# Column sums in a Sinkhorn loop: two 256-column products of split operands in place of one fp32 product

## The chip, the core and the metric

One core of a Trainium2 chip runs the whole kernel. The metric is the device time in microseconds, the median of several runs. The core has five engines that run side by side, each its own queue in order: TensorE (PE; its weight loads are shown apart as PEld), VectorE (DVE), ScalarE (ACT), GpSimd (POOL) and SyncE (SP), which issues transfers. SBUF is the on-chip memory; TensorE writes to PSUM, which VectorE and ScalarE read.

## What is computed

A linear attention feeds a first mixture of experts (soft slots), and that a second one, whose gates a Sinkhorn loop evens out. The change touches only the loop:

```python
def _moe2_ref(x, w_gate, w1, w2):
    N, D = x.shape                      # 2304 tokens, 512 features
    E = w_gate.shape[1]                 # 8 experts
    logits = x @ w_gate
    P = np.exp(logits - logits.max())
    for _ in range(8):
        P /= P.sum(1, keepdims=True) + 1e-09     # rows
        P /= P.sum(0, keepdims=True) + 1e-09     # columns
        P *= N / E
    out = np.zeros((N, D))
    for e in range(E):
        h = np.maximum(x @ w1[e], 0.0)
        out += P[:, e:e + 1] * (h @ w2[e])
    return out
```

## The kernel before

The second mixture is TensorE's long part. It goes through 8 experts, and in each through 9 blocks of 256 tokens (the loop over `blocks`, L1247). A block of an expert is 7 products (`product`, L1170, the seven of a fast scheme for block matrices), each of 12 matmuls with a 256-column moving operand, and behind the third product the first layer of the next block: 4 matmuls into PSUM tile `z1`, then 4 into `z0` (`first_layer`, L1077). `hidden` (L1088) makes the seven operands of the next block from these two tiles in five steps, one behind each product: ScalarE and VectorE form sums and rounded parts (`s`, `hh_s`, `hh_a`, `hl_a`), and GpSimd forms the rests of four sums (`lo_s`, L1107: `hl_s`, 128x512, two pairs a block). `take` (L1189) adds the finished products into `xo`; in the first expert ScalarE copies some of them and VectorE adds the others. GpSimd also prepares the next expert's weights (`w_t`, `w_b`, `moe_w`, 128x1024, by the tables `W_SUMS` and `W_PARTS`, L1243): one such operation stands behind the sixth step of most blocks, after the second pair of `hl_s`.

The gates `P` stand in SBUF as 128 partitions x 18 token tiles x 8 experts. They are wanted only when the first expert ends, so the Sinkhorn loop (`sinkhorn`, L1021) is a generator whose steps are strewn into the first expert's blocks: `SINK_0` for block 0 and `SINK` for the others (L1245). With `SINK = {1: 3, 5: 2}` one pass of the loop spans two blocks: behind product 5 (counted from 0) of a block VectorE multiplies `P` by the reciprocal row sums and reduces it over its 18 tiles to `cs`, 128x8. Behind product 1 of the next block TensorE adds `cs` over the partitions and repeats the sum on all of them by a product with a matrix of ones (L1067, PSUM tile `pcs`); VectorE reads it, inverts, multiplies `P` and takes the next row sums. Pass 0 has its row and column sums at the end of block 0, in one stretch. The tile `pcs` is the buffer of `z0` in passes 0 to 6. In pass 7 the next expert's `make_stack` and `spread_stack` (L991, L1009) fall in the same block: TensorE makes `ps`, VectorE splits it into `st` (a copy and a subtraction), and TensorE spreads it by the products `pr` just ahead of `pcs`.

What sets the order is the program text: all engines are wrapped in `InOrder` (L43), so each queue runs its instructions as the code names them. `gst` (L1220, 128x8, rounded fp32) holds the gate's operand, which is used up when the loop begins; `pad` (L477) is an unused tile of 8 elements.

Of the kernel before, what the change touches and what calls it, by code (L numbers as in the profile page):

```python
# [7 lines left out]
F32 = mybir.dt.float32  # L8
F32R = mybir.dt.float32r
AF = mybir.ActivationFunctionType  # L10
ALU = mybir.AluOpType
# [7 lines left out]
E, SPE, FF = 8, 4, 1024  # L19
# [35 lines left out]
def tile_kernel(ctx: ExitStack, tc: tile.TileContext, a):  # L55
    nc = tc.nc
    PE, V, A, G, SP = nc.tensor, nc.vector, nc.scalar, nc.gpsimd, nc.sync

    const = ctx.enter_context(tc.tile_pool(name="const", bufs=1, side="left"))
# [8 lines left out]
    def load_const(name, shape, pool=None, q=SP):  # L68
        t = (pool or const).tile(shape, F32, name=name, bufs=1)
        q.dma_start(out=t, in_=a[name])  # L70
        return t
# [62 lines left out]
    def load_k(t):  # L134
        x = kp.tile([128, 512], F32, tag="kt", name=f"kt{t}", bufs=4)
        SP.dma_start(out=x, in_=a["kT"][t])
        kt_t[t] = x
# [336 lines left out]
    load_k(2)  # L474
    load_v(1)
    load_k(3)
    const.tile([128, 8], F32, name="pad", bufs=1)  # L477
    wg = const.tile([128, KC, E], F32, name="wg", bufs=1)
    ct4 = const.tile([128, 256], F32R, name="ct4", bufs=1)
    ident = load_const("ident", [128, 128])  # L480
    ones = load_const("ones", [128, 128])
# [16 lines left out]
    PE, V, A, SP, G = (InOrder(tc, x) for x in (PE, V, A, SP, G))  # L498
# [189 lines left out]
    def old_sums(c):  # L688
# [14 lines left out]
        out=dg, in0=ident[0:NS, 0:NS].unsqueeze(1).to_broadcast([NS, 3, NS]), scalar1=mx[0:NS], scalar2=-1.0,  # L703
# [18 lines left out]
    for h in range(2):  # L722
        ps = mm(f"psit{h}", (F0, P1)[h])
        for c in range(2):
            for n in range(2):
                for g in range(2):
                    r = slice(g * 64, (g + 1) * 64)
                    PE.matmul(
                        ps[r, c * NS:(c + 1) * NS], x_t[NT - 2 + n][:, h * 256 + c * 128:h * 256 + (c + 1) * 128][:, r], ee[:, n, :],
                        start=c + n == 0, stop=n == 1, skip_group_check=True,  # L730
# [220 lines left out]
    for g in range(4):  # L951
        r = slice(32 * g, 32 * g + 32)
# [25 lines left out]
    cp = ctx.enter_context(tc.tile_pool(name="cp", bufs=1, side="right", reuse_waits="tile"))  # L978
# [6 lines left out]
    def acc_tile(name):  # L985
        return pm.tile([128, 512], F32, tag="m", name=name)

    def z_tile(n, name):
        return pz.tile([128, 1024], F32, tag=f"z{n}", name=name)
# [31 lines left out]
    def sinkhorn():  # L1021

        pg = acc_tile("pgate")
        for c in range(KC):
            for g in range(2):
                r = slice(g * 64, (g + 1) * 64)
                PE.matmul(pg[r, 0:8 * E].rearrange("p (r e) -> p r e", r=8), sot[:, c, r], wg[:, c, :].unsqueeze(1).to_broadcast([128, 8, E]), start=c == 0, stop=c == KC - 1)
        V.tensor_copy(out=gst, in_=pg[:, 0:E])
        V.tensor_tensor(out=gst[64:128, :], in0=pg[64:128, 0:E], in1=gst[64:128, :].bitcast(F32), op=ALU.subtract)
        yield  # L1030
        pl = acc_tile("plog")
        for t in range(NT):
            PE.matmul(
                pl[:, t * E:(t + 32) * E].rearrange("p (r e) -> p r e", r=32),
                ct[t // 4][:, t % 4 * 128:(t % 4 + 1) * 128], gst.unsqueeze(1).to_broadcast([128, 32, E]),
                start=True, stop=True, skip_group_check=True,
            )
            if t in (7, 13):
                yield
        yield  # L1040
        V.tensor_copy(out=P, in_=pl[:, 0:NT * E].rearrange("p (t e) -> p t e", e=E))
        gm, gm1 = gmt[:, 0:1], gmt[0:1, 1:2]
        V.tensor_reduce(out=gm, in_=pl[:, 0:NT * E], axis=AX.X, op=ALU.max)
        G.memset(PE1[:, :, E:E + 1], 1e-9)
        yield
        pg = acc_tile("pgm")
        PE.transpose(pg[0:1, 0:128], gm, ident)
        V.tensor_reduce(out=gm1, in_=pg[0:1, 0:128], axis=AX.X, op=ALU.max)
        yield
        PE.matmul(pg[:, 128:129], ones[0:1, :], gm1, start=True, stop=True)  # L1050
        yield
        V.tensor_scalar_mul(gm, pg[:, 128:129], -1.0)
        A.activation(out=P, in_=P, func=AF.Exp, bias=gm)
        yield
        for it in range(8):
            rs = cp.tile([128, NT, 1], F32, tag="rs", name=f"rs{it}")
            V.tensor_reduce(out=rs, in_=PE1, axis=AX.X, op=ALU.add)
            V.reciprocal(out=rs, in_=rs)
            yield
            V.tensor_tensor(out=P, in0=P, in1=rs.to_broadcast([128, NT, E]), op=ALU.mult)  # L1060
            yield
            cs = cp.tile([128, 1, E], F32, tag="cs", name=f"cs{it}")
            csf = cs.rearrange("p o e -> p (o e)")
            V.tensor_reduce(out=csf, in_=P.rearrange("p t e -> p e t"), axis=AX.X, op=ALU.add)
            yield
            pg = z_tile(0, f"pcs{it}") if it < 7 else acc_tile(f"pcs{it}")
            PE.matmul(pg[:, 0:E], ones, csf, start=True, stop=True)  # L1067
            V.tensor_scalar(out=csf, in0=pg[:, 0:E], scalar1=1e-9, scalar2=float(E) / NTOK, op0=ALU.add, op1=ALU.mult)
            V.reciprocal(out=csf, in_=csf)
            yield  # L1070
            V.tensor_tensor(out=P, in0=P, in1=cs.to_broadcast([128, NT, E]), op=ALU.mult)
            yield
# [144 lines left out]
    sums = {}  # L1217
    blocks = [(e, blk) for e in range(E) for blk in range(NBLK)]
    sink = sinkhorn()
    gst = cp.tile([128, E], F32R, name="gst")  # L1220
    gmt = cp.tile([128, 2], F32, name="gm")
# [120 lines left out]
```

## Time and profile before

| | us |
|---|---|
| runs | 995.48, 990.32, 994.38 |
| median | 994.38 |
| the profiled execution | 995.96 |
| its span, first to last instruction | 994.1 |
| outside its span | 1.9 |

The busy shares of the span are TensorE 99%, VectorE 69%, GpSimd 60%, ScalarE 56%. The first expert of the second mixture lies between about 214 and 310 us, the eight passes between 227 and 310 us, the other seven experts behind. How to read the rows: a row of the timeline is one instruction or a run of like ones (x2), with its start from the span's beginning and its length; where the engine was idle before, the row ends with the time and with what ended it. A row's length holds all that the instruction waited for after it was issued. Neighbouring rows of an engine may overlap by some 0.05 to 0.1 us.

### The profile page before, as it was taken

To read this page: it belongs to the slowest core of one execution; us is meant where nothing else is said; L and a number is where in the kernel's file an instruction comes from. 1 tells how busy PE (TensorE), PEld (TensorE's weight loads), DVE (VectorE), ACT (ScalarE), POOL (GpSimd) and SP (SyncE) were. 2 spreads that over 40 slices of the span, in tenths; PEclk is the share of its full clock that TensorE was granted. 3 is DMA by queue.
4 is the path that set the end of the run, shared out by engine and by line. 5 is a ranking of instruction groups with operands and counts; after the bars stand their busy time and mean duration, and the time that the engine had idled before them with its cause. 6 is when DMAs were issued, how large, how long until landed. Compare 5 with 4: busy or idle time off the path is not lost.

```text
span 994.1 us, 28051 instructions
## 1 busy us (share of the span) xinstructions
PE 980.6 (99%) x11698; PEld 935.7 (94%) x11698; DVE 688.8 (69%) x1360; ACT 556.5 (56%) x1018; POOL 593.7 (60%) x462
## 2 busy tenths in 40 slices
PE   8899999999999999999999999999999999999998
PEld 7899987569999999999999999999999999999998
DVE  6778766277886766676766776676676677667675
ACT  5566554265657666655564555554654565555452
POOL 2122220055678677867786678678777777787443
PEclk9999999999999999999999999999999999999999
DMA  8777578980003100310040004000400130001111
GB/s 238 219 239 221 170 244 301 393 303 2 1 1 128 44 1 1 128 44 2 1 156 16 1 1 170 2 2 20 151 2 1 66 106 1 2 1 38 49 44 64
DMA packets 29517, 88.84 MB, mean 89 GB/s; under 512 B 3920, under 2 KB 6864, under 8 KB 24144
## 3 DMA queue, kind: packets, MB, share of 16 engines
q1 hardware_dynamic: 20560, 68.05, 20.0%
q10 hardware_dynamic: 8640, 18.88, 5.9%
q8 instruction: 92, 1.51, 0.6%
q14 instruction: 33, 0.27, 0.1%
q0 software_dynamic: 192, 0.13, 0.1%
HBM read 82.33 MB, written 4.72 MB: 88 GB/s over the span
## 4 chain that ended last, share of the span: by engine, by line
PE 96%; DMA 1%; DVE 1%; issue 1%; ACT 1%; DVEq 0%; ACTq 0%
PE x L51 39%; PE y L51 20%; PE z L51 16%; PE kvacc L51 4%; PE num L51 3%; PE pq L51 2%; PE pk L51 2%; PE ut L51 2%; DMA moe_w<-in_moe_w 1%; PE ps L51 1%; PE ph L51 1%; PE po L51 1%; PE xt L51 1%; PE lg L51 1%; PE xl L51 1%
## 5 line engine op out<-in xcount | busy, mean ns | idle before, releaser
L51 POOL TENSOR_TENSOR hl_s<-s,hh_s 128x512 fp32r<-128x512 f32 x286 | 365.5, 1300 | 205.7 <-ACT hh_s L51 189.6
L51 PE MATMUL x<-w_t,hh_s 128*128 128x256 f32 x1152 | 204.7, 278 | 0.1
L51 ACT ACTIVATE hh_s<-s 128x512 fp32r<-128x512 f32 x287 | 174.9, 630 | 50.6 <-PE x L51 26.3
L51 ACT ACTIVATE r<-z 128x512 f32<-128x512 f32 x143 | 85.8, 600 | 163.0 <-PE z L51 162.3
L51 PEld LDWEIGHTS x<-w_t,hh_s 128*128 128x128 f32 x1152 | 173.4, 188 | 1.1 <-ACT xo L51 0.3
L51 DVE SCALAR_TENSOR_TENSOR xo<-x,P,xo 128x256 f32<-128x256 f32 x252 | 120.9, 480 | 68.3 <-PE x L51 66.7
L51 ACT ACTIVATE hh_a<-z 128x512 fp32r<-128x512 f32 x216 | 122.2, 600 | 73.2 <-DVE s L51 71.7
L51 PE MATMUL x<-w_t,hl_s 128*128 128x256 f32 x576 | 158.7, 276 | 0.0
L51 DVE SCALAR_TENSOR_TENSOR s<-z,r 128x512 f32<-128x512 f32 x143 | 98.0, 685 | 84.6 <-ACT hh_a L51 80.7
L51 DVE SCALAR_TENSOR_TENSOR hl_a<-z,hh_a 128x512 fp32r<-128x512 f32 x216 | 147.1, 681 | 2.7 <-ACT hh_a L51 2.7
L51 PEld LDWEIGHTS x<-w_t,hl_s 128*128 128x128 f32 x576 | 107.9, 188 | 0.0
L51 PE MATMUL z<-w_b,hh_a 128*128 128x256 f32 x576 | 102.4, 278 | 0.0
L51 PE MATMUL y<-w_b,hh_s 128*128 128x256 f32 x576 | 101.7, 276 | 0.0
L51 PE MATMUL x<-w_t,hh_a 128*128 128x256 f32 x576 | 101.6, 276 | 0.0
L51 PE MATMUL y<-w_t,hh_s 128*128 128x256 f32 x576 | 101.6, 276 | 0.0
L51 PE MATMUL x<-w_b,hh_a 128*128 128x256 f32 x576 | 101.3, 276 | 0.0
L51 DVE SCALAR_TENSOR_TENSOR s<-z,s 128x512 f32<-128x512 f32 x143 | 97.7, 684 | 3.9 <-POOL hl_s L51 2.1
L51 PEld LDWEIGHTS z<-w_b,hh_a 128*128 128x128 f32 x576 | 86.6, 188 | 2.9 <-issue 2.9
L51 PEld LDWEIGHTS y<-w_b,hh_s 128*128 128x128 f32 x576 | 86.8, 188 | 0.0
L51 PEld LDWEIGHTS x<-w_t,hh_a 128*128 128x128 f32 x576 | 86.8, 188 | 0.0
L51 PEld LDWEIGHTS y<-w_t,hh_s 128*128 128x128 f32 x576 | 86.8, 188 | 0.0
L51 PEld LDWEIGHTS x<-w_b,hh_a 128*128 128x128 f32 x576 | 86.6, 188 | 0.0
(211 smaller groups left out, 1982.7 us busy)
## 6 DMA issues: line engine op xcount, KB each, us to landing
moe_w<-in_moe_w SPq DMA_DIRECT2D x41, 1024.0 KB, 6.9
moe_w<-in_moe_w ACTq DMA_DIRECT2D x48, 256.0 KB, 3.7
moe_w<-in_moe_w ACTq DMA_DIRECT2D x12, 512.0 KB, 5.3
vs<-in_vb SPq DMA_DIRECT2D x20, 256.0 KB, 4.2
kt<-in_kT SPq DMA_DIRECT2D x18, 256.0 KB, 4.1
qt<-in_qT SPq DMA_DIRECT2D x18, 256.0 KB, 3.4
half<-in_moe_w SPq DMA_DIRECT2D x8, 512.0 KB, 6.6
out<-xo SPq DMA_DIRECT2D x18, 128.0 KB, 1.7
```

What stands on the lines that cost most here:

```text
L51: return lambda *args, **kwargs: self.tc.keep_in_program_order(make(*args, **kwargs))
```

## The change

The product of `cs` with ones in fp32 goes. In its place VectorE rounds `cs` to a narrower format (`csh`, in place of the tile `pad`) and stores the rest `cs - csh` into `gst`. TensorE multiplies both parts with a rounded copy of the ones, `onesr`, into one sum. Each part is read 32 times over, so that the moving operand has 256 columns of which eight are used. `onesr` is a new tile of the pool `cp` and is written once, by VectorE, in the step of the generator that also does the first row sums. For that pool the tiles besides `rs` and `cs` come to lie 512 bytes lower in each partition.

```diff
-    const.tile([128, 8], F32, name="pad", bufs=1)
+    csh = const.tile([128, E], F32R, name="csh", bufs=1)
...
         A.activation(out=P, in_=P, func=AF.Exp, bias=gm)
         yield
+        onesr = cp.tile([128, 128], F32R, tag="onesr", name="onesr")
+        V.tensor_copy(out=onesr, in_=ones)
         for it in range(8):
...
             V.tensor_reduce(out=csf, in_=P.rearrange("p t e -> p e t"), axis=AX.X, op=ALU.add)
+            V.tensor_copy(out=csh, in_=csf)
+            V.tensor_tensor(out=gst, in0=csf, in1=csh.bitcast(F32), op=ALU.subtract)
             yield
             pg = z_tile(0, f"pcs{it}") if it < 7 else acc_tile(f"pcs{it}")
-            PE.matmul(pg[:, 0:E], ones, csf, start=True, stop=True)
+            for n in range(2):
+                PE.matmul(
+                    pg[:, 0:256].rearrange("p (r e) -> p r e", r=32), onesr,
+                    (csh, gst)[n].unsqueeze(1).to_broadcast([128, 32, E]), start=n == 0, stop=n == 1,
+                )
```

On VectorE, pass 1 (blocks 1 and 2) read before:

```order
L51 TENSOR_TENSOR P<-P,rs_4434 128x18x8
L51 TENSOR_REDUCE cs_4536<-P 128x8
L51 SCALAR_TENSOR_TENSOR hl_a_2_4528<-z_0_2_4450,hh_a_2_4526 128x512
L51 TENSOR_TENSOR xo<-z_4573,xo 128x256
L51 TENSOR_SCALAR cs_4536<-pcs_4587 128x8
L51 RECIPROCAL cs_4536<-cs_4536 128x8
L51 TENSOR_TENSOR P<-P,cs_4536 128x18x8
L51 TENSOR_REDUCE rs_4592<-P 128x18
```

and reads now:

```order
L51 TENSOR_TENSOR P<-P,rs_4439 128x18x8
L51 TENSOR_REDUCE cs_4541<-P 128x8
L51 CAST csh<-cs_4541 128x8
L51 TENSOR_TENSOR gst<-cs_4541,csh 128x8
L51 SCALAR_TENSOR_TENSOR hl_a_2_4533<-z_0_2_4455,hh_a_2_4531 128x512
L51 TENSOR_TENSOR xo<-z_4580,xo 128x256
L51 TENSOR_SCALAR cs_4541<-pcs_4594 128x8
L51 RECIPROCAL cs_4541<-cs_4541 128x8
L51 TENSOR_TENSOR P<-P,cs_4541 128x18x8
L51 TENSOR_REDUCE rs_4600<-P 128x18
```

The copy and the subtraction stand between the reduction and `hl_a`; all else keeps its place.

On TensorE, in block 8 around pass 7's product, it read before (the fp32 product is one row here and two instructions in the trace):

```order
L51 MATMUL pr_1_5551<-st_5530,rep 128x256 x2
L51 MATMUL pr_0_5550<-st_5530,rep 128x256 x2
L51 MATMUL pr_1_5551<-st_5530,rep 128x256 x2
L51 MATMUL pcs_5565<-cs_5479,ones 128x8
L51 MATMUL x_5499<-w_t_4035,hh_s_8_5448 128x256 x2
```

and reads now:

```order
L51 MATMUL pr_0_5575<-st_5555,rep 128x256 x2
L51 MATMUL pr_1_5576<-st_5555,rep 128x256 x2
L51 MATMUL pr_0_5575<-st_5555,rep 128x256 x2
L51 MATMUL pr_1_5576<-st_5555,rep 128x256 x2
L51 MATMUL pcs_5590<-csh,onesr 128x256
L51 MATMUL pcs_5590<-gst,onesr 128x256
L51 MATMUL x_5524<-w_t_4035,hh_s_8_5471 128x256 x2
```

One row has become two in the same place; no other row of TensorE moves.

## Rows read from the trace of the kernel before

**Rows 1.** The page's first part: busy us (share of the span) xinstructions

```profile
PE 980.6 (99%) x11698; PEld 935.7 (94%) x11698; DVE 688.8 (69%) x1360; ACT 556.5 (56%) x1018; POOL 593.7 (60%) x462
```

**Rows 2.** Stretches: length; busy PE, PEld, DVE, ACT, POOL; clock, DMA, GB/s

```profile
227.00:309.00 82.00, 82.00 (x730) 80.68 (x730) 66.12 (x130) 48.14 (x100) 57.33 (x38) 1.00 0.03 9
325.00:425.00 100.00, 100.00 (x900) 98.68 (x899) 69.75 (x135) 64.08 (x109) 74.27 (x50) 1.00 0.15 50
```

**Rows 3.** Timeline (start, length, engine, line, operation, tiles, shapes, count): loads, products

```profile
211.40 0.97 PEld L51 LDWEIGHTS plog<-gst,ct 128*128 128x128 f32 x8 [0.41 <-issue]
...
230.12 0.28 PE L51 MATMUL pcs<-cs,ones 128*128 128x8 f32 x2
...
241.06 0.31 PEld L51 LDWEIGHTS pcs<-cs,ones 128*128 128x128 f32 x2
...
241.18 0.29 PE L51 MATMUL pcs<-cs,ones 128*128 128x8 f32 x2
...
251.85 0.28 PE L51 MATMUL pcs<-cs,ones 128*128 128x8 f32 x2
```

**Rows 4.** Timeline at 142 us: VectorE's small instructions and GpSimd's two

```profile
141.95 0.57 DVE L51 TENSOR_TENSOR mx<-mx,mx 128x1 f32<-128x1 f32 x1
142.63 0.48 DVE L51 TENSOR_SCALAR dg<-ident,mx 32x32 f32<-32x32 f32 x1
143.03 0.14 DVE L51 TENSOR_TENSOR al<-mx,mx 128x1 f32<-128x1 f32 x1
...
141.89 1.18 POOL L51 TENSOR_TENSOR xx<-nums,rd 128x256 f32<-128x256 f32 x2 [3.14 <-DVE rd L51]
```

**Rows 5.** Timeline of pass 1: VectorE and GpSimd

```profile
239.31 0.44 DVE L51 TENSOR_REDUCE cs<-P 128x8 f32<-128x144 f32 x1
...
242.22 1.99 DVE L51 TENSOR_TENSOR P<-P,cs 128x144 f32<-128x144 f32 x1
...
239.09 2.58 POOL L51 TENSOR_TENSOR hl_s<-s,hh_s 128x512 fp32r<-128x512 f32 x2 [0.76 <-DVE s L51]
...
240.38 1.29 POOL L51 TENSOR_TENSOR hl_s<-s,hh_s 128x512 fp32r<-128x512 f32 x1
...
241.62 2.41 POOL L51 TENSOR_TENSOR w_b<-moe_w,w_b 128x1024 fp32r<-128x1024 f32 x1
```

**Rows 6.** Groups by form, VectorE: shapes xcount | busy us, mean ns | idle before

```profile
L51 DVE CAST cst<-lg 128x128 fp32r<-128x128 f32 x8 | 1.4, 223 | 0.1
...
L51 DVE CAST cst<-lg 128x64 fp32r<-128x64 f32 x2 | 0.3, 191 | 1.2 <-PE pc L51 1.2
```

**Rows 7.** Timeline: a load that waited for VectorE, and GpSimd in pass 2

```profile
223.92 0.27 DVE L51 TENSOR_REDUCE gm<-pgm 1x1 f32<-1x128 f32 x1
...
224.24 0.29 PEld L51 LDWEIGHTS pgm<-gm,ones 1*128 1x128 f32 x2 [0.41 <-DVE gm L51]
...
251.35 1.27 POOL L51 TENSOR_TENSOR hl_s<-s,hh_s 128x512 fp32r<-128x512 f32 x1
```

**Rows 8.** Timeline of pass 0: VectorE and GpSimd's second operation

```profile
227.85 0.31 DVE L51 TENSOR_REDUCE rs<-P 128x18 f32<-128x162 f32 x1
...
228.50 0.31 DVE L51 TENSOR_TENSOR P<-P,rs 128x144 f32<-128x144 f32 x1
...
228.66 1.30 POOL L51 TENSOR_TENSOR hl_s<-s,hh_s 128x512 fp32r<-128x512 f32 x1
```

**Rows 9.** Timeline of pass 7: VectorE, GpSimd's second operation, TensorE

```profile
304.76 0.67 DVE L51 SCALAR_TENSOR_TENSOR hl_a<-z,hh_a 128x512 fp32r<-128x512 f32 x1
...
306.76 0.42 DVE L51 CAST st<-ps 128x256 fp32r<-128x256 f32 x1 [0.99 <-PE ps L51]
307.22 0.42 DVE L51 TENSOR_TENSOR st<-ps,st 128x256 fp32r<-128x256 f32 x1
...
305.49 1.28 POOL L51 TENSOR_TENSOR hl_s<-s,hh_s 128x512 fp32r<-128x512 f32 x1
...
308.23 0.51 PE L51 MATMUL pr<-st,rep 32*128 32x256 f32 x8
```

## The prediction

> **What bounds the kernel now.** I read the page's busy table first, then busy time by stretches, then the timelines of the eight Sinkhorn passes (numbered 0 to 7 here). TensorE is busy for 980.6 of 994.1 us [rows 1], and in the stretch that holds all passes, 227 to 309 us, for 82.00 of 82.00 us at a granted clock of 1.00 (2.4 GHz); after it no idle time is left to win a delay back [rows 2]. VectorE is busy for 66 and GpSimd for 57 of those 82 us. So work that the change gives to VectorE costs nothing until TensorE has to wait for it, and each such wait goes straight into the time.
>
> **TensorE's own work.** The fp32 product runs as two passes of 8 columns, each with its weight load. The two loads take 0.31 us where one takes 0.19, so the second begins 0.12 us after the first [rows 3]. The new pair is two products of 256 columns, also with two loads. Such products exist: eight `plog` products, `gst` repeated 32 times, whose loads take 0.97 us, 0.19 and seven steps of 0.11 [rows 3]. The load sets the step in both: **0 us**, within 0.01 a step. The Trainium skill, "TensorE: Matmul & The Clock Gate", section "Back-to-back issue gap", gives an isolated product of up to 64 columns about 60 cycles and one of 256 columns 262; by that table alone 16 products would cost some 1.3 us more (an estimate from that page). The rows decide here, since they hold the loads.
>
> **A second tempo.** Between the products of passes 0 and 1 lie 11.06 us, between those of 1 and 2 only 10.67 [rows 3], with the same 94 products in each: steps of 0.118 and of 0.1135 us. Of the six periods up to pass 6 three are long, three short, and the change falls on the 8-column pair, whose short products shift loads against products. With products of one length I see no reason for a switch; which tempo stays, no row says. I take the quick one, that of the long stretch behind (900 recorded products in 100 us [rows 2]): **-3 x 0.39 = -1.17 us**; were all slow, +1.17.
>
> **VectorE's added work.** Two instructions a pass on 8 elements: a copy that rounds and a subtraction. The nearest row is the subtraction of one element, `al`, 0.14 us [rows 4]: 8 x 2 x 0.14 = 2.2 us, and one copy of 128x128. VectorE has that room. The danger is not their length but **GpSimd**. `mx`, an instruction of two inputs and one element like `al`, took 0.57 us because it began 0.06 us after the first of two GpSimd operations (1.18 us together, so the first ends at 142.48). It ended 0.04 us behind the first, while the second ran; then `dg`, with one SBUF input and two values beside it, was caught behind the second and took 0.48 us, again ending 0.04 us behind it. `al`, after both, took 0.14 [rows 4]. So such an instruction waits for the running GpSimd operation, gets in before the next, and its successor is caught again. `P<-P,cs` shows the same in the passes: 1.99 us, to 0.18 us behind the end of `w_b`. The reduction `cs` isn't held, 0.44 us beside a running GpSimd [rows 5].
>
> The subtraction has two inputs in SBUF, as `mx` has. Whether the copy is held, no row shows, since none meets a GpSimd operation; its bounds are 0 and the rest of that operation. Nearest to it: copies of this kind, `cst`, take 191 ns for 64 elements and 223 for 128 [rows 6], 0.5 ns an element, where `P<-P,rs` against `al` (0.31 for 144, 0.14 for 1) gives 1.2 [rows 4, 8]. They move two elements in the time of one. And `dg`, which has one tensor input as a copy has, was held. I take: held. The Trainium skill, "SBUF — State Buffer", section "SBUF: two separate sides", says that a VectorE instruction in a two-port mode or with two SBUF inputs and a GpSimd operation exclude each other for a whole instruction, and "VectorE: DVE Perf Modes", section "Mode 2×_2P — use both read ports for one tensor", names `tensor_copy` among the two-port ones. By these pages the copy waits, and the time is the forecast, not rival 1; `mx` and `dg` agree with the first, with 0.57 and 0.48 us.
>
> **Passes 1 to 6.** In pass 1 `cs` is reduced from 239.31 to 239.75. GpSimd has just begun two `hl_s` operations, 239.09 to 240.38 and 240.38 to 241.67, with `w_b` queued behind [rows 5]. The copy is held to 240.42; the subtraction asks at about 240.45, meets the second `hl_s` and ends at 241.67 + 0.04 = 241.71. TensorE starts 0.05 us later (`gm` ended at 224.19, the load that waited for it began at 224.24 [rows 7]): 241.76. Its second load of the pair stands at 241.18: **0.58 us**. In pass 2 the second `hl_s` ends at 251.35 + 1.27 = 252.62 [rows 7], TensorE could go at 252.71 and is there at 251.85: **0.86 us**. Passes 3 and 6 are like 1, 4 and 5 like 2; the tempo makes the difference, as GpSimd's pair hangs on TensorE's fourth product of a block, five products ahead. With the quick tempo all six cost 0.86: 6 x 0.86 - 1.17 = **3.99 us**; with the tempos of now 4.32, with the slow one 6 x 0.58 + 1.17 = 4.65. The wait doesn't shrink from block to block, since GpSimd's operations follow TensorE's first layer and shift with it.
>
> What is queued behind the blocked subtraction on VectorE: `hl_a`, `xo<-z`, the read of `pcs`, the reciprocal, `P<-P,cs`. `hl_a` reads `z1`, which the next first layer overwrites: it would end at 241.71 + 0.67 = 242.4, and TensorE comes there 13 steps after 241.76, at 243.2. These 0.8 us are its cover; what exceeds them would be paid in each pass. `P<-P,cs` waits for `w_b` till 244.03 anyway [rows 5], so there the queue has caught up.
>
> **Pass 0.** The big copy stands ahead of the first row sum, at 227.85. GpSimd's `hl_s` changes at 228.66 and ends at 229.96 [rows 8]. The copy, held, ends at 228.70. From the sum to `P<-P,rs` are 0.65 us: it asks at 229.35, where it now slips in at 228.50, and ends at 229.96 + 0.18 = 230.14. Then `cs`, copy and subtraction, 0.43 + 0.14 + 0.14 with gaps of 0.03: 230.94, TensorE at 230.99 where its second load stands at 230.12 [rows 3]: **0.87 us**. A copy that isn't held is late enough, too.
>
> **Pass 7.** Its product comes 3 us after the sums, but on VectorE `hl_a`, `xo<-x` and two `st` instructions queue behind the subtraction, which ends at 305.49 + 1.28 + 0.04 = 306.81. `hl_a` begins 0.08 earlier, as `al` did before `dg`'s end: 306.73, 1.97 later than now. `st` has 0.99 us idle time before it; the last one ends 0.98 later, at 308.62. `pr`, now at 308.23, needs it: 308.67, **0.44 us** [rows 9].
>
> **Sum.** 0.87 + 3.99 + 0.44 = 5.30 us. The profiled run would be 995.96 + 5.30 = 1001.3 (span 999.4); it lies 1.6 us above the median, and from that it is 994.38 + 5.30 = **999.7 us**. Bounds: 4.4 if weights load during the wait (8 steps of 0.11 less), 6.0 with the slow tempo; with the scatter of the runs (990.32 to 995.48), 996 to 1002.
>
> **Rivals.** (1) *No second hold, not slower.* The copy isn't held, or the subtraction gets in before the second `hl_s`: it asks 0.07 us after that row's start, and the point is whether GpSimd has the way by then. For it: the margin. Against: `mx` was caught after 0.06 us, and `dg` right after `mx`. Passes 1 to 7 then cost nothing: 0.87 - 1.17, so 994.1 us. (2) *Held by the third as well.* If `w_b` went ahead of the waiting subtraction, that would end 2.4 us later in six passes: 999.7 + 14.4 = 1014. Against: `mx` got in between two queued operations. (3) *The layout.* `onesr` takes 512 bytes a partition, and the other tiles of its pool move by as much. If TensorE's tempo hung on addresses, 1% of the 680 us behind would be 6.8 us either way: 987 or 1006. No row shows such a link; both tempos occur on the same tiles.
>
> **How the numbers follow.** The forecast has 0.66, rival 1 0.20, rival 2 0.05, rival 3 0.03 each way; 0.03 is left for what I don't see. A measurement tells about 0.5% (5 us) from no change. The forecast lies on that line: of its 0.66 I give 0.38 to slower, 0.28 to the same. Slower 0.38 + 0.05 + 0.03 + 0.02 = 0.48, same 0.28 + 0.19 = 0.47, faster 0.05. The range takes in the forecast and rival 1 with a run's scatter: 992 to 1002.8.
>
> **What would show it.** Right: the copy at about 0.6 and `gst` at 1.2 to 1.3 us on VectorE in passes 1 to 6; TensorE idle six times for 0.5 to 0.9 us with `gst` as releaser; `P<-P,rs` of pass 0 at 0.8; products of neighbouring passes about 11.5 us apart. Wrong: `gst` at 0.14 in every pass (rival 1), at 3.6 (rival 2), or another step than 0.1135 us after 325 (rival 3).

## The result

The changed kernel takes 999.26 us, the median of seven runs (996.85 to 1005.46), against 994.38 us for the kernel before (seven runs, 990.32 to 995.93). The ratio is **1.0063 with a 95% interval of 1.0041 to 1.0086**: 4.1 to 8.6 us more, where the two medians alone lie 4.9 us apart. It is slower by more than the measurement is uncertain, and the line of 0.5% lies inside the interval. The four longest of the seven runs list a granted clock of 0.997 to 0.999 and the three shortest (996.85 to 997.42 us) one of 1.000, which the profiled execution has too; whether that has to do with the change, no run shows.

The profiled execution of the changed kernel took 996.85 us, the lowest of its seven, and its span of 995.0 us is only 0.9 us longer than that of before. In that execution the part ahead of the loop ran 4.7 us quicker: 230.12 less 226.32, plus pass 0's delay of 0.92, worked out below. This part scatters: in the nine profiled kernels of this study, with almost the same program up to there, the first `pcs` comes at any time between 226.32 and 231.48 us. So I compare stretches of the trace and not spans. From the second load of pass 0's `pcs` to the end of the span before took 994.1 - 230.12 = 763.98 us, the changed kernel 995.0 - 226.32 = 768.68: 4.70 us more, and pass 0's own delay, which lies ahead of that point, comes on top.

### The profile page after: what moved, and what is told of

It reads as the page before. It is cut to its first block, busy times and chain, and to the rows that moved or that the text cites. A ratio compares the mean times of both kernels' runs of the same rounds, so it can differ in the third digit from the quotient of the medians.

```text
span 995.0 us, 28069 instructions
## 1 busy us (share of the span) xinstructions
PE 981.8 (99%) x11698; PEld 935.7 (94%) x11698; DVE 697.9 (70%) x1377; ACT 556.6 (56%) x1018; POOL 593.8 (60%) x462
## 4 chain that ended last, share of the span: by engine, by line
PE 91%; POOL 3%; DVE 3%; issue 2%; ACT 1%; POOLq 0%; DVEq 0%; ACTq 0%
PE x L51 36%; PE y L51 18%; PE z L51 15%; PE kvacc L51 4%; PE num L51 3%; POOL hl_s L51 3%; PE pq L51 2%; PE pk L51 2%; PE ut L51 2%; PE ph L51 2%; PE po L51 1%; PE ps L51 1%; DVE gst L51 1%; DVE s L51 1%; PE xt L51 1%
```

## The profile after

The page's busy line, then its chain by engine (shares of the span).

```profile
PE 981.8 (99%) x11698; PEld 935.7 (94%) x11698; DVE 697.9 (70%) x1377; ACT 556.6 (56%) x1018; POOL 593.8 (60%) x462
...
PE 91%; POOL 3%; DVE 3%; issue 2%; ACT 1%; POOLq 0%; DVEq 0%; ACTq 0%
```

Against [rows 1], TensorE has as many instructions as before and VectorE 17 more, 9.1 us of them busy, which is more than their work (16 x 0.17 and 0.22, as will be seen): it holds their waits. In the chain that ends last GpSimd and VectorE now have 3% each; before, VectorE had 1% and GpSimd nothing.

Busy time by stretches (length; busy PE, PEld, DVE, ACT, POOL; clock, DMA, GB/s), shifted by 4 us against [rows 2] as the passes are.

```profile
223.00:305.00 82.00, 78.99 (x668) 77.66 (x667) 71.05 (x138) 45.95 (x97) 52.40 (x36) 1.00 0.01 1
325.00:425.00 100.00, 100.00 (x900) 98.68 (x899) 69.69 (x134) 63.69 (x108) 75.11 (x50) 1.00 0.14 47
```

Where TensorE was busy without a gap it is now idle for 3 of 82 us at a granted clock of 1.00; behind the passes nothing has changed. What it waits for, by engine, tile and releaser (sum of us, times, longest), from 216 to 325 us:

```profile
PEld pcs L51 <- DVE gst L51: 3.5, 6, 0.8
...
PE pcs L51 <- DVE gst L51: 2.3, 6, 0.6
...
PEld pcs L51 <- issue: 0.8, 1, 0.8
...
PE pcs L51 <- DVE csh L51: 0.7, 1, 0.7
...
PE pr L51 <- DVE st L51: 0.4, 1, 0.4
```

Six waits for `gst` (passes 1 to 6), one for `csh` (pass 0), one for `st` (pass 7). None of them stands among the waits of the kernel before. Pass 1 in the timeline (start, length, engine, operation), VectorE, GpSimd and TensorE's loads:

```profile
235.39 0.44 DVE L51 TENSOR_REDUCE cs<-P 128x8 f32<-128x144 f32 x1
235.87 0.68 DVE L51 CAST csh<-cs 128x8 fp32r<-128x8 f32 x1
236.58 1.20 DVE L51 TENSOR_TENSOR gst<-cs,csh 128x8 fp32r<-128x8 f32 x1
...
235.17 2.58 POOL L51 TENSOR_TENSOR hl_s<-s,hh_s 128x512 fp32r<-128x512 f32 x2 [0.76 <-DVE s L51]
237.72 2.38 POOL L51 TENSOR_TENSOR w_b<-moe_w,w_b 128x1024 fp32r<-128x1024 f32 x1
...
236.77 0.19 PEld L51 LDWEIGHTS z<-w_b,hl_a 128*128 128x128 f32 x1
...
237.83 0.19 PEld L51 LDWEIGHTS pcs<-gst,onesr 128*128 128x128 f32 x1 [0.76 <-DVE gst L51]
```

The two `hl_s` end at about 236.46 (half of 2.58) and 237.75. The copy ends at 236.55, just behind the first; the subtraction asks at 236.58 and ends at 237.78, just behind the second, although `w_b` was already queued. TensorE's load follows 0.05 us later. This is the course that the prediction wrote out from [rows 4, 5].

Pass 0, the same engines:

```profile
223.15 0.83 DVE L51 CAST onesr<-ones 128x128 fp32r<-128x128 f32 x1
...
224.55 0.87 DVE L51 TENSOR_TENSOR P<-P,rs 128x144 f32<-128x144 f32 x1
...
225.90 0.17 DVE L51 CAST csh<-cs 128x8 fp32r<-128x8 f32 x1
226.10 0.17 DVE L51 TENSOR_TENSOR gst<-cs,csh 128x8 fp32r<-128x8 f32 x1
...
222.60 2.65 POOL L51 TENSOR_TENSOR hl_s<-s,hh_s 128x512 fp32r<-128x512 f32 x2 [0.76 <-DVE s L51]
...
225.17 0.19 PEld L51 LDWEIGHTS z<-w_b,hl_a 128*128 128x128 f32 x1
226.18 0.19 PEld L51 LDWEIGHTS pcs<-csh,onesr 128*128 128x128 f32 x1 [0.83 <-issue]
226.32 0.19 PEld L51 LDWEIGHTS pcs<-gst,onesr 128*128 128x128 f32 x1
```

The big copy is held by the first `hl_s` to 223.98 (they change at 223.93), `P<-P,rs` by the second to 225.42, where before it slipped in with 0.31 us [rows 8]. The small copy and the subtraction meet no GpSimd operation and take 0.17 us each. From the last `z` load to the second `pcs` load are 1.15 us; before they were 0.23 (229.89 to 230.00 and one step of 0.12):

```profile
229.89 0.19 PEld L51 LDWEIGHTS z<-w_b,hl_a 128*128 128x128 f32 x1
230.00 0.30 PEld L51 LDWEIGHTS pcs<-cs,ones 128*128 128x128 f32 x2
```

Pass 7, the last `st` and TensorE's loads of `pr`:

```profile
308.57 0.42 DVE L51 TENSOR_TENSOR st<-ps,st 128x256 fp32r<-128x256 f32 x1
...
309.11 0.33 PEld L51 LDWEIGHTS pr<-st,rep 32*128 32x128 f32 x8 [0.54 <-PE z L51]
```

TensorE waits until `st` is there (308.99); before, `pr` did not wait [rows 9].

Where the passes stand, read off the timeline: the time between the second loads of `pcs` of neighbouring passes, the stretch from pass 0 to 6, and what follows pass 7's (all in us, read to within 0.04):

| kernel | 0-1 | 1-2 | 2-3 | 3-4 | 4-5 | 5-6 | 6-7 | 0 to 6 | after 7 |
|---|---|---|---|---|---|---|---|---|---|
| before | 11.06 | 10.68 | 11.05 | 10.68 | 10.71 | 11.05 | 13.44 | 65.23 | 685.31 |
| changed | 11.51 | 11.50 | 11.62 | 11.65 | 11.61 | 11.63 | 13.84 | 69.52 | 685.32 |
| e1_no_rest | 11.06 | 11.06 | 10.67 | 10.65 | 10.71 | 10.65 | 13.45 | 64.81 | 685.51 |
| e2_vector_pair_only | 11.06 | 10.67 | 11.06 | 10.68 | 10.70 | 11.06 | 13.87 | 65.23 | 686.73 |
| e3_gpsimd_halves | 11.38 | 11.26 | 11.38 | 11.38 | 11.27 | 11.26 | 13.77 | 67.93 | 685.12 |
| e4_sums_in_psum | 11.05 | 11.06 | 11.06 | 11.06 | 11.06 | 11.06 | 13.73 | 66.35 | 685.36 |
| e5_psum_and_early_ones | 10.67 | 11.10 | 11.06 | 11.06 | 11.06 | 11.06 | 13.73 | 66.01 | 685.32 |
| e6_ones_copy_only | 11.04 | 10.69 | 11.06 | 10.68 | 10.70 | 11.06 | 13.43 | 65.23 | 686.77 |
| e7_s3_rest_on_vector | 10.66 | 13.95 | 12.57 | 10.66 | 13.93 | 10.67 | 15.55 | 72.44 | 685.03 |

The loss sits where it was expected: 4.29 us from pass 0 to 6, 0.40 between 6 and 7, 0.92 ahead of pass 0's product, 0.01 behind pass 7. Together 5.6 us, inside the 4.1 to 8.6 us of the runs.

## The experiments

The theory: each of the two new VectorE instructions is held for the whole GpSimd operation that runs when it asks, gets in ahead of the next, and so is late twice. Its rivals: the wide products themselves cost the time; VectorE's longer queue costs it, held or not; the new tile's place in memory costs it. Runs of one kernel scatter by 5.6 to 8.6 us, so all but one of these runs are read by the table above and by their instructions.

**`e1_no_rest`: no rest, wide products kept.** The rest is left out: `csh` is multiplied twice and the sum halved, so the column sums are those of rounded numbers.

```diff
             V.tensor_copy(out=csh, in_=csf)
-            V.tensor_tensor(out=gst, in0=csf, in1=csh.bitcast(F32), op=ALU.subtract)
...
-                    (csh, gst)[n].unsqueeze(1).to_broadcast([128, 32, E]), start=n == 0, stop=n == 1,
+                    csh.unsqueeze(1).to_broadcast([128, 32, E]), start=n == 0, stop=n == 1,
...
```

> Changed kernel without the subtraction: both 256-column products read the rounded part csh, and the sum is halved afterwards, so the rest of the column sums is left out. Theory (the subtraction is held by GpSimd's second hl_s and TensorE waits for it): csh still about 0.68 us in passes 1 to 6, but ready 0.6 us ahead of its product, so no wait of TensorE there; second loads of pcs from pass 0 to pass 6 together 64.0 to 66.4 us (before 65.2, changed 69.5), no wait ahead of pr in pass 7. Pass 0 keeps about 0.7 us, since the copy of the ones and the held P<-P,rs stay. Rival A (the two wide products themselves cost TensorE the time): still 69.5 us. Rival B (the length of VectorE's added instructions counts, one of two is gone): about 67.4 us.

Measured 996.63 us, one run. Pass 1, VectorE and TensorE's loads:

```profile
240.68 0.68 DVE L51 CAST csh<-cs 128x8 fp32r<-128x8 f32 x1
...
241.84 0.19 PEld L51 LDWEIGHTS z<-w_b,hl_a 128*128 128x128 f32 x1
241.96 0.30 PEld L51 LDWEIGHTS pcs<-csh,onesr 128*128 128x128 f32 x2
242.19 0.30 PEld L51 LDWEIGHTS x<-w_t,hh_s 128*128 128x128 f32 x2
```

The copy is held (0.68 us) and TensorE doesn't notice: the pair of wide products takes 0.23 us, as the fp32 pair does (0.22 in the rows of the next run), and all delay in passes 1 to 6 is gone: 64.81 us is two slow and four quick periods (2 x 11.06 + 4 x 10.67) and no wait. So the wide products cost nothing, and one hold is hidden; the second is not. Only pass 0's wait stays (0.6 us, for `csh`), and pass 7 has none, 13.45 against 13.44.

**`e2_vector_pair_only`: VectorE's pair alone, fp32 product kept.** The copy and the subtraction run, nobody reads their results, and `onesr` isn't made.

```diff
...
             V.tensor_reduce(out=csf, in_=P.rearrange("p t e -> p e t"), axis=AX.X, op=ALU.add)
+            V.tensor_copy(out=csh, in_=csf)
+            V.tensor_tensor(out=gst, in0=csf, in1=csh.bitcast(F32), op=ALU.subtract)
             yield
```

> Kernel before with VectorE's copy and subtraction put in, their results unused; the fp32 product stays and needs only cs. No copy of the ones. Theory: VectorE shows csh 0.68 and gst 1.20 us in passes 1 to 6 as in the changed kernel, yet TensorE has no wait there: 65.2 us from pass 0 to pass 6 (64.0 to 66.4 with either tempo); pass 7 keeps 0.4 us ahead of pr, whose st queues behind the pair. Rival B (VectorE's longer queue is the cost): 69 us or so. Rival A (wide products): 65.2 us as well, so this run tells against B only.

Measured 995.97 us, one run. Pass 1:

```profile
237.93 0.67 DVE L51 CAST csh<-cs 128x8 fp32r<-128x8 f32 x1
238.64 1.21 DVE L51 TENSOR_TENSOR gst<-cs,csh 128x8 fp32r<-128x8 f32 x1
...
239.21 0.31 PEld L51 LDWEIGHTS pcs<-cs,ones 128*128 128x128 f32 x2
239.43 0.30 PEld L51 LDWEIGHTS x<-w_t,hh_s 128*128 128x128 f32 x2
```

Both holds are there at full length, and with them VectorE's delayed queue, yet passes 0 to 6 take 65.23 us as before: TensorE goes on at 239.21 while the subtraction still waits until 239.85. What costs time in passes 1 to 6 is that TensorE needs the held result, not that VectorE stands. Pass 7 is the exception that the prediction made: there `st` is late by VectorE's queue alone, `pr` waits 0.4 us for it, and 6-7 takes 13.87 (13.84 with the whole change). In pass 0 the copy asks while GpSimd's last operation runs and takes 0.68 us; the subtraction finds GpSimd idle and takes 0.17.

**`e3_gpsimd_halves`: GpSimd's operations halved.** Each `hl_s` of block 1 onward is cut into two of half the size; the rest of the change stays.

```diff
+            if 0 < i < NBLK:
+                for c in range(2):
+                    r = slice(2 * c, 2 * c + 2)
+                    G.tensor_tensor(out=l[:, r], in0=s[:, r], in1=h[:, r].bitcast(F32), op=ALU.subtract)
+                return
```

> Changed kernel; in blocks 1 to 8 of the first expert each hl_s of GpSimd is made in two operations of half the size, the same work in twice as many instructions. Theory (a VectorE instruction is held for one whole GpSimd operation and gets in before the next): gst falls from 1.20 to about 0.6 us, TensorE's wait in passes 1 to 6 from 0.5 to 0.9 to 0 to 0.25 us each, pass 0 to 6 together 64.0 to 66.7 us. If GpSimd and VectorE merely share a way and slow each other, gst stays near 1.2 us and it is 69.5 us. Rivals A and B: 69.5 us, since neither the products nor VectorE's instructions change. Pass 0 should be cheaper too: P<-P,rs waits for half an operation, 0.3 to 0.6 us instead of 0.87.

Measured 997.46 us, one run. Pass 1, VectorE and GpSimd:

```profile
238.01 0.88 DVE L51 TENSOR_TENSOR P<-P,rs 128x144 f32<-128x144 f32 x1
...
239.40 0.17 DVE L51 CAST csh<-cs 128x8 fp32r<-128x8 f32 x1
239.61 0.60 DVE L51 TENSOR_TENSOR gst<-cs,csh 128x8 fp32r<-128x8 f32 x1
...
237.98 2.89 POOL L51 TENSOR_TENSOR hl_s<-s,hh_s 128x256 fp32r<-128x256 f32 x4 [0.61 <-ACT hh_s L51]
```

Half an operation is 0.72 us (2.89 for four). The subtraction asks at 239.61 and ends at 240.21, just behind the third half (240.15): 0.60 us in this and all other passes, half of 1.20. The hold's length is that of the GpSimd operation. The total is a miss: 67.93 us from pass 0 to 6 where I had expected 64.0 to 66.7. The first half begins 0.03 us before `P<-P,rs` asks, where in the changed kernel the whole operation began 0.11 us after it (235.17 and 235.06). So it catches `P<-P,rs` as well (0.88 us instead of 0.30), the sums begin 0.58 us later and TensorE still waits seven times, 2.2 us in all. Pass 0 got cheaper, as expected, but by another course: neither the copy of the ones (0.22 us) nor `P<-P,rs` (0.31) is held there, only the subtraction (0.60).

**`e4_sums_in_psum`: sums in PSUM.** The reduction writes its sums into unused columns of the PSUM tile that holds `y`; copy and subtraction read them there.

```diff
-            V.tensor_reduce(out=csf, in_=P.rearrange("p t e -> p e t"), axis=AX.X, op=ALU.add)
-            V.tensor_copy(out=csh, in_=csf)
-            V.tensor_tensor(out=gst, in0=csf, in1=csh.bitcast(F32), op=ALU.subtract)
+            sm = whole[it, "y"][:, 256:256 + E]
+            V.tensor_reduce(out=sm, in_=P.rearrange("p t e -> p e t"), axis=AX.X, op=ALU.add)
+            V.tensor_copy(out=csh, in_=sm)
+            V.tensor_tensor(out=gst, in0=sm, in1=csh.bitcast(F32), op=ALU.subtract)
...
```

> Changed kernel; VectorE's column reduction writes to a free half of the PSUM bank of tile y, and the copy and the subtraction read it from there, so the copy has no input in SBUF and the subtraction one. Theory: neither is held any more (st<-ps of this form took 0.42 us beside a running GpSimd), csh and gst 0.16 to 0.18 us each in all passes, no wait of TensorE in passes 1 to 7, pass 0 to 6 together 64.0 to 66.4 us; pass 0 keeps its 0.9 us. That would be the changed kernel less 4 to 5 us. Rivals A and B: 69.5 us.

Measured 995.93 us, one run. VectorE and GpSimd in pass 1:

```profile
238.32 0.17 DVE L51 CAST csh<-y 128x8 fp32r<-128x8 f32 x1
238.52 0.17 DVE L51 TENSOR_TENSOR gst<-y,csh 128x8 fp32r<-128x8 f32 x1
...
237.62 2.59 POOL L51 TENSOR_TENSOR hl_s<-s,hh_s 128x512 fp32r<-128x512 f32 x2 [0.76 <-DVE s L51]
```

Both instructions run in the middle of the first `hl_s` and take 0.17 us; in all eight passes the subtraction takes 0.166 to 0.167. Same instructions, same sizes, same place in the queue: only the source has moved out of SBUF, and the hold is gone, TensorE's waits at `pcs` with it except pass 0's. The stretch still takes 66.35 us, because now all six periods have the slow tempo (6 x 11.06), which is no wait of TensorE's.

**`e5_psum_and_early_ones`: sums in PSUM and the big copy earlier.** As the run before, and `onesr` is made ahead of the second mixture, at 210.5 us, where GpSimd has been idle for 6 us.

```diff
-        onesr = cp.tile([128, 128], F32R, tag="onesr", name="onesr")
-        V.tensor_copy(out=onesr, in_=ones)
         for it in range(8):
...
     gmt = cp.tile([128, 2], F32, name="gm")
+    onesr = cp.tile([128, 128], F32R, name="onesr")
+    V.tensor_copy(out=onesr, in_=ones)
```

> The run before (column sums in PSUM) with the copy of the ones moved ahead of the second mixture, where no Sinkhorn step waits for it. Theory: all of the changed kernel's cost is gone. P<-P,rs of pass 0 slips in as in the kernel before (0.31 us), no wait of TensorE at pcs or pr. With no wait and no 8-column pair the tempo should stay as it is at pass 0, quick: 64.0 us from pass 0 to pass 6, 1.2 less than before (with the slow one 66.4, 1.1 more). Time 993 to 996 us beside before at 994, so the same within what can be told, and 4 to 6 us under the changed kernel. Rivals A (wide products), B (VectorE's length) and the layout: as slow as the changed kernel, 0.4 to 0.8% over before.

Measured 995.02 us, the median of 11 runs (992.81 to 998.43), against 995.38 for the kernel before beside it (15 runs): ratio 0.9997, interval 0.9981 to 1.0013. No difference shows; by the interval, 1.3 us more or 1.9 less stay possible. The tiles `csh`, `gst` and `onesr` (count; shortest/median/longest ns; first and last start):

```profile
L51 DVE CAST csh<-y x8: 165/167/168, 229.0 to 305.6; 128x8 fp32r<-128x8 f32 x8
...
L51 DVE TENSOR_TENSOR gst<-y,csh x8: 165/166/167, 229.2 to 305.8; 128x8 fp32r<-128x8 f32 x8
...
L51 DVE CAST onesr<-ones x1: 216/216/216, 210.5 to 210.5; 128x128 fp32r<-128x128 f32 x1
```

The copy of the ones takes 0.22 us here and 0.83 in the changed kernel. TensorE waits at no `pcs` and no `pr`. With both holds gone and the copy of the ones made early, the loss is gone within what the runs can tell, while the wide products stay. The tempo was not as expected: not quick, with 64.0 us from pass 0 to 6, but slow from pass 1 on, with 66.01, 0.78 more than before.

**`e6_ones_copy_only`: the copy of the ones alone.** The kernel before with `onesr` made and not used; the pool's tiles move by its 512 bytes as in the change.

```diff
         yield
+        onesr = cp.tile([128, 128], F32R, tag="onesr", name="onesr")
+        V.tensor_copy(out=onesr, in_=ones)
         for it in range(8):
```

> Kernel before with the copy of the ones alone, at its place in the changed kernel and unused; this also moves the pool's tiles by 512 bytes as the change does. Theory: onesr 0.83 us and P<-P,rs 0.87 in pass 0; the product needs only cs there, so TensorE waits about 0.6 us once; pass 0 to pass 6 65.2 us as before, and behind 325 us steps of 0.1133 us: the layout costs nothing. Layout rival: another step behind 325 us, or 5 us somewhere else.

Measured 995.26 us, one run. Pass 0, VectorE and TensorE's loads:

```profile
224.84 0.83 DVE L51 CAST onesr<-ones 128x128 fp32r<-128x128 f32 x1
...
226.23 0.87 DVE L51 TENSOR_TENSOR P<-P,rs 128x144 f32<-128x144 f32 x1
...
226.79 0.19 PEld L51 LDWEIGHTS z<-w_b,hl_a 128*128 128x128 f32 x1
227.65 0.30 PEld L51 LDWEIGHTS pcs<-cs,ones 128*128 128x128 f32 x2 [0.68 <-issue]
```

From the last `z` load to the second load of `pcs`, 0.12 behind 227.65, are 0.98 us, 0.75 more than before: most of pass 0's 0.92 comes from this copy, the rest from the two small instructions. The passes behind keep 65.23 us, with their tempos in the same order. So the layout costs nothing there; what follows pass 7 takes 1.4 us more than before, in one stretch of slow tempo of about 35 us (656 to 691), and `e2_vector_pair_only`, which has no such tile, loses as much (686.73) in such a stretch at another place (850 to 884). In the changed kernel there is none (685.32).

**`e7_s3_rest_on_vector`: a different operation behind the first.** In blocks 1 to 7 VectorE makes the second rest of the pair itself, so that the subtraction meets whatever GpSimd has next; the rest of the change stays.

```diff
-            (G if i or name != "s1" else V).tensor_tensor(out=l, in0=s, in1=h.bitcast(F32), op=ALU.subtract)
+            (V if i == 0 and name == "s1" or 0 < i < NBLK - 1 and name == "s3" else G).tensor_tensor(out=l, in0=s, in1=h.bitcast(F32), op=ALU.subtract)
```

> Changed kernel; in blocks 1 to 7 of the first expert VectorE forms the rest of s3, not GpSimd, so GpSimd's second hl_s of the late pair is gone and its weight operation of 2.4 us comes next. Theory: the copy is still held by the first hl_s (0.68 us), the subtraction then by whatever GpSimd runs next. Where that is a sum of weights, ready at once (passes 2, 3, 5), gst takes about 2.4 us and TensorE waits 1.6 to 2 us; where it first needs ScalarE's rounded weights (passes 1, 4, 6), gst slips in at 0.17 us and TensorE doesn't wait. So fewer operations on GpSimd, and yet longer waits in three passes. Rival (GpSimd's load as such counts): all six waits shrink, as GpSimd has 1.3 us less to do in each block.

Measured 1006.31 us, one run. VectorE and GpSimd in passes 1 and 2:

```profile
241.02 0.69 DVE L51 CAST csh<-cs 128x8 fp32r<-128x8 f32 x1
241.74 0.17 DVE L51 TENSOR_TENSOR gst<-cs,csh 128x8 fp32r<-128x8 f32 x1
...
242.42 2.57 DVE L51 TENSOR_TENSOR hl_s<-s,hh_s 128x512 fp32r<-128x512 f32 x1
...
253.05 0.68 DVE L51 CAST csh<-cs 128x8 fp32r<-128x8 f32 x1
253.76 2.27 DVE L51 TENSOR_TENSOR gst<-cs,csh 128x8 fp32r<-128x8 f32 x1
...
242.05 2.39 POOL L51 TENSOR_TENSOR w_b<-moe_w,w_b 128x1024 fp32r<-128x1024 f32 x1 [0.38 <-ACT w_b L51]
...
253.67 2.34 POOL L51 TENSOR_TENSOR moe_w<-moe_w 128x1024 f32<-128x1024 f32 x1
```

In pass 1 GpSimd waits for ScalarE between its operations, and the subtraction takes 0.17 us. In pass 2 `moe_w` starts at 253.67, 0.09 us before the subtraction asks, and holds it to 256.03: 2.27 us, one operation of 2.34. Over the passes 1 to 6 the lengths are 0.17, 2.27, 2.27, 0.17, 2.27 and 0.17. Neither a fixed price of 1.2 us nor VectorE's length gives this; one whole GpSimd operation does, whichever it is. The long periods of the table are those that end at passes 2, 3 and 5. Against the expectation TensorE also waits behind passes 1, 4 and 6, where the subtraction slipped in. There the weight operation holds VectorE's own `hl_s` instead (2.57 us from 242.42; 0.67 in pass 2, where GpSimd stands idle by then), the read of `pcs` stands behind it in the queue and begins at 245.25, and the first layer, which writes that buffer, waits for the read (3.0 us in three waits).

## Why the prediction was right, and where not

**TensorE's own work, 0 us: right.** The wide pair took 0.23 us and so did the fp32 pair, and in `e1_no_rest` a quick period took 10.65 to 10.71 us where before it took 10.68 to 10.71. By the table of isolated products in the Trainium skill, "TensorE: Matmul & The Clock Gate", section "Back-to-back issue gap", the sum would have been 1.3 us higher; the trace doesn't agree, and the weight loads, 0.11 us apart, set the step.

**The holds, 0.58 and 0.86 us a pass: right.** The copy took 0.68 and the subtraction 1.20 us. Against before's periods of like tempo (10.67 and 11.06), passes 1 and 2 came 0.84 and 0.83 us later, passes 3 to 6 by 0.55 to 0.59. That the copy is held was the one link without a row; `e1_no_rest` and `e2_vector_pair_only` show it alone. The Trainium skill, "SBUF — State Buffer", section "SBUF: two separate sides", has a VectorE instruction in a two-port mode or with two SBUF inputs and a GpSimd operation exclude each other for a whole instruction; the trace agrees, with 0.60 us against halves of 0.72, 1.20 against operations of 1.29, and 2.27 against one of 2.34. Rival 1 falls with the second hold, rival 2 with `gst` at 1.20 us while `w_b` was queued, rival 3 with the unchanged stretch behind pass 7 (its lower time, 987, is counted from the time before; from the forecast it would have been 993).

**Pass 0, 0.87 us: 0.92. Pass 7, 0.44 us: 0.40.** In pass 0 the two small instructions took 0.17 us each instead of 0.14. The mechanisms are shown by `e6_ones_copy_only` and `e2_vector_pair_only`, each alone.

**The second tempo, -1.17 us: wrong.** The step that failed is "with products of one length I see no reason for a switch", and with it the choice of the quick tempo. The changed kernel goes quick in the first two periods and slow in the next four: 2 x 10.67 + 4 x 11.055 = 65.56 us without waits, 0.33 more than before instead of 1.17 less. In `e5_psum_and_early_ones`, whose products have all one length and where no wait stands at `pcs`, the tempo falls from quick to slow at the `pcs` of pass 1, behind a single step of 0.15 us between two loads, and stays there up to pass 7. The price of it was covered: with the slow tempo the waits are shorter, as the prediction said, 0.57 instead of 0.86. So passes 1 to 6 came to 69.52 - 65.56 = 3.96 us of waits and 0.33 of tempo, 4.29 in place of 3.99. The two errors, 5.16 of waits foreseen against 3.96 and 1.17 gained against 0.33 lost, nearly cancel, and the sum is 5.6 in place of 5.30. That they cancel is only in part luck: a slow period costs 0.39 us and takes some 0.27 off the wait at its end (0.84 and 0.57).

The forecast stood on the line between slower and the same; the runs, which scatter by 9 us for the changed kernel, put it just beyond, with the line still inside the interval. With such a scatter it is in part luck that the median, 999.26 us, came within 0.5 us of the forecast.

## What to carry to other kernels

An instruction that looks free by its 0.17 us can cost a whole operation of another engine: before giving VectorE a copy or a two-input step in SBUF, look in the timeline at what GpSimd runs at that moment and what is queued behind it, and count one hold for each dependent step. A hold costs only where someone waits for its result; one was hidden here, the second was not. Where operands can come from PSUM, as the sums here, or the step can stand where GpSimd is idle, the hold goes away.

## What the runs showed of the hardware

- A waiting VectorE instruction gets in between two queued GpSimd operations, but its dependent successor, which asks 0.03 us after its end, is too late and is held by the next. The reduction took 0.44 us beside a running GpSimd and 0.41 where it stood idle (pass 0), and both instructions with their source in PSUM took 0.17 us beside it: none of them was held.
- TensorE's stream of 256-column products has two tempos at a granted clock of 1.00, about 0.1133 and 0.1178 us a product. In the kernel before, `e2_vector_pair_only` and `e6_ones_copy_only`, which share the fp32 pair, they follow each other in the same order up to pass 6. With the wide pair the order is another in each kernel: mostly quick in `e1_no_rest`, all slow in `e4_sums_in_psum`, changing at a `pcs` in `e5_psum_and_early_ones`. Behind pass 7 a change needs no `pcs` either: in `e6_ones_copy_only` the slow stretch begins behind a single step of 0.22 us at 655.5 and ends at the products `ps`. Neither the products' lengths alone nor a wait alone decides it, and what does stays open. The most that it can move from pass 0 to 6 is 6 x 0.39 = 2.3 us.
